# An attention block with a gated SwiGLU on one Trainium2 core: the first head's start reordered, and half of the normalised rows transposed by DMA

## The chip, the cores and the metric

The kernel runs on one core of a Trainium2 chip. The metric is the device time of an execution in microseconds (us). The core has TensorE (PE in the profile; PEld is its weight load), VectorE (DVE), ScalarE (ACT), GpSimd (POOL) and SyncE (SP), which here only issues transfers. Each engine takes its instructions in order, and engines wait for each other by semaphores. DMA transfers are issued from the queues of SP, ACT and POOL.

## The reference

A layer norm of x (2048 rows of 640) feeds an attention with 32 heads of 192 columns over a cache of 2048 keys, and a SwiGLU with 1536 hidden columns. The output joins the two:

```python
xn = _layernorm(x, axis=-1)
q = (xn @ wq).reshape(B, Sq, H, Dh).transpose(0, 2, 1, 3)
scores = jnp.einsum("bhqd,bhkd->bhqk", q, k_cache) * (Dh ** -0.5)
o = jnp.einsum("bhqk,bhkd->bhqd", softmax(scores), v_cache)
s = o.transpose(0, 2, 1, 3).reshape(B, Sq, H * Dh) @ wo
ffn = (silu(xn @ w1) * (xn @ w3)) @ w2
return x + s * silu(ffn)
```

All operands are bfloat16.

## The kernel before

**Stages.** First comes the layer norm of the 16 row tiles (128 rows each), of which tiles 0 to 3 are done before anything else and the rest inside head 0. Then the 32 heads run one after the other; each head also projects the queries of the next head. At the end come the rest of the SwiGLU and the output product. The change touches the start and head 0 only.

**Layer norm.** `ln_stats(i)` (L179) takes mean and variance of tile i on DVE; `ln_sums` (L186) does so for tiles 1 and 4 on ACT. `ln_root(i0)` (L196) makes the inverse deviations of tiles i0 and i0+1 on ACT, from the statistics of both. `ln_scale(i0)` (L214) scales the two tiles on DVE into `xn`. A *turn*, `ln_turn(i0)` (L224), transposes the two tiles on PE, ten 128x128 products by an identity into a PSUM tile `pst`, and returns the two copies from there into `xnT` (columns are rows of x); `next_turn` (L233) makes the copies on ACT.

**Projection.** `project_chunk(h, qb)` (L268) makes the queries of head h for block qb, which is 512 rows of x, or four tiles; so it needs two turns' worth of `xnT`. Head 0 uses full products of 128 rows; later heads use pairs of 64 rows, with `xnS`, a copy of `xnT` with its row halves exchanged (`swap_rows`, L298, two DMAs on POOL's queue). The PSUM tile `ps` is cast into `qA` and `qF` (DVE in head 0, ACT for head 0's first chunk and for head 1), and POOL makes `qS`, which is `qA` with its halves exchanged, and `qD` (L289, L290). `maxima()` takes the largest absolute values, from which a bound on the scores is made: DVE multiplies them with the keys' maxima and POOL sums over partitions (`bound`, L322). The bound of the very first block is made by `first_bound` (L309), with a product on PE.

**Attention.** A head has 4 blocks of 8 *pairs* of key tiles; (q, p) is pair p of block q. `advance` (L432) does one pair: `scores` (L361, six products in three steps: `qA` with `KA`, `qS` with `KB` and `KC`, `qD` and `qF` with `KC` and `KB`) into a PSUM tile, one exponential of 1024 columns on ACT (`weights`, L375) with the bound `nb` as bias, and the products with the values in two half pairs (`values`, L406; eight products each), which are queued in `parts` and lag behind by up to four halves. At the end of a block DVE reads the output banks (`evict`, L380).

**PSUM.** Scores, projections and turns share one tag, `st2`, with two buffers, which they take in program order. So the scores of a pair wait until the user two places earlier has been read: by its exponential, its casts or its copies.

**What stands where in head 0.** `advance` takes an `extra`, run on PE between pairs: before, turns at pairs 3 and 4 of block 0 (1 and 3 of blocks 1 and 2), head 0's next chunk at pair 5 (4), head 1's chunk at pair 7 (6; 1 in block 3). `posts` (L475) names layer norm steps that follow a pair. `pin` keeps an instruction's place in program order on its engine; others may be moved by the scheduler.

**Loads.** `load_keys(h)` (L102) issues on SP two transposing DMAs of the keys (`KA`, `KB`, columns 0 to 127 and 64 to 191) and the values. `load_weights(h)` (L86) issues three DMAs, for head 0 from ACT, for later heads from POOL. `copy_keys` (L116) makes `KC` on POOL by two copies and sets a column of the values to 1. `keep_busy(n)` (L175) runs n products on constants, to no other end than to keep PE busy.

Of the kernel before, what the change touches and what calls it, by code (L numbers as in the profile page):

```python
# [30 lines left out]
def _kernel_impl(ctx, tc, A_x, A_k_cache, A_v_cache, A_wq, A_wo, B_w1, B_w3, B_w2, out):  # L31
# [70 lines left out]
    def load_keys(h, mid=None):  # L102
        kh = A_k_cache[0, h]
# [3 lines left out]
        for K, c in ((KA, 0), (KB, DH - P)):  # L107
            for r in ((slice(0, HALF), slice(HALF, SK)) if h == 0 else (slice(0, SK),)):
                nc.sync.dma_start_transpose(out=K[:, r], in_=kh[r, c:c + P])  # L109
            if mid and K is KA:  # L110
                mid()
        vt = kvp.tile([P, NKT, DH + 2], BF16, tag="vt")
        nc.sync.dma_start(out=vt[:, :, 0:DH], in_=vh.rearrange("(t p) d -> p t d", p=P))
# [14 lines left out]
    with ExitStack() as actx:  # L128
# [32 lines left out]
        def load_x(eng, t0, t1):  # L161
            eng.dma_start(out=x_all[:, t0:t1, :], in_=x2[t0 * P:t1 * P, :].rearrange("(t p) d -> p t d", p=P))
# [70 lines left out]
        def next_turn(i0):  # L233
            for copy in ln_turn(i0):
                copy()

# [15 lines left out]
        keep_busy(2)  # L252
# [3 lines left out]
        def start_head(h):  # L256
            L = loads.pop(h)
            heads[h] = dict(
                h=h, L=L, vt=L["vt"],
# [8 lines left out]
        def project_chunk(h, qb, cast=nc.vector.tensor_copy):  # L268
# [21 lines left out]
            keep(nc.gpsimd.tensor_copy(out=qD[:, qs], in_=qF[PGW:P, qs]))  # L290
# [18 lines left out]
        def first_bound():  # L309
# [4 lines left out]
                                               in1=hd["st"][:, 2:4, 0], op0=ALU.mult, op1=ALU.mult))  # L314
            bp = ps_o.tile([P, 2, 512], F32, tag="ob0", name="bp")
# [45 lines left out]
        def scores(hd, qb, p):  # L361
# [7 lines left out]
            for s, step in enumerate(steps):  # L369
                for t, (k, ks, q) in enumerate(step):  # L370
# [35 lines left out]
        def values(hd, qb, p, pT2):  # L406
            vt = hd["vt"]
# [34 lines left out]
        start_head(0)  # L442
        loads[1] = load_weights(1)
        ln_sums(4)
        for s in range(2):
            for k in range(2):
                key_maxima(0, s, k, 2)
        maxima = project_chunk(0, 0, nc.scalar.copy)
        swap_rows(0)
        loads[1].update(load_keys(1))  # L450
        maxima()
        early = [scores(heads[0], 0, p) for p in range(2)]
        keep_busy(2)
        first_bound()
        keep_busy(4)
        ln_stats(5)
# [3 lines left out]
        start_head(1)  # L460
# [3 lines left out]
        def first_project(h, qb):  # L464
            maxima = project_chunk(h, qb, nc.vector.tensor_copy if h == 0 else nc.scalar.copy)
# [6 lines left out]
        def steps(*fs):  # L472
# [3 lines left out]
            (0, 1): ((ln_root, 4), (ln_stats, 6), (ln_scale, 4), (ln_stats, 7)),  # L476
            (0, 3): ((ln_root, 6), (ln_scale, 6), (ln_stats, 8), (ln_stats, 9)),
# [369 lines left out]
```

## Time and profile before

| | us |
|---|---|
| median of 3 runs (lowest, highest) | 1953.76 (1953.71, 1954.74) |
| profiled execution, its own time | 1953.86 |
| its span, first to last instruction | 1952.0 |
| PE busy in the span | 1937.1 |
| first exponential of head 0 starts | 20.92 |
| first values of head 0 start | 22.36 |
| mean granted PE clock (1 is full speed) | 0.999 |

The three costliest waits of PE in the whole span are these (columns: us in total, times, longest):

```profile
PE st L371 <- POOL qS L289: 2.2, 2, 1.9
PE fill L177 <- DVE cols L144: 1.6, 1, 1.6
PE pst L228 <- DVE xn L220: 1.5, 2, 0.9
```

An arrow points at what ended the wait. In a timeline line the first two numbers are start and duration, "x10" counts merged instructions, and brackets hold the idle time before them with what ended it. PE's durations overlap, as matmuls are pipelined; the distance between two starts says how long one occupied PE. Off the PE, a long idle time costs nothing by itself.

### The profile page before, as it was taken

How to read it: one execution, taken by the hardware profiler on the slowest of the kernel's cores; microseconds unless marked ns; L12 is line 12 of the kernel's file. 1: busy time of each engine (PE TensorE's matmuls, PEld its weight loads, DVE VectorE, ACT ScalarE, POOL GpSimd, SP SyncE). 2: the span in 40 equal slices, each digit the busy share in tenths (PEclk: the TensorE clock that was granted, in tenths of full speed). 3: DMA queues.
4: the chain of work that ended last, by engine and by line, in shares of the span. 5: the costliest groups of instructions: out<-in, count | busy, mean ns of one | idle time of the engine just before them, and what ended most of it. 6: DMA issues, size and time to landing. Idle time of an engine off the chain costs nothing.

```text
span 1952.0 us, 60577 instructions
## 1 busy us (share of the span) xinstructions
PE 1937.1 (99%) x27276; PEld 1331.6 (68%) x27276; DVE 1139.0 (58%) x2262; ACT 1219.0 (62%) x1192; POOL 441.6 (23%) x642
## 2 busy tenths in 40 slices
PE   8999999999999999999999999999999999999998
PEld 4676666667766666666666666666666666567775
DVE  7765656676666666666666666666665655531111
ACT  6777777676777777777777777777777777210000
POOL 3422222222222222222222222222222210000000
PEclk9999999999999999999999999999999999999999
DMA  9332222222233322232323222323232203938882
GB/s 208 80 83 36 73 40 71 52 70 57 60 67 63 68 63 68 56 85 64 76 54 76 54 76 46 84 46 84 46 74 38 57 10 112 269 77 137 155 153 55
DMA packets 352938, 153.52 MB, mean 79 GB/s; under 512 B 303824, under 2 KB 345776, under 8 KB 352672
## 3 DMA queue, kind: packets, MB, share of 16 engines
q1 hardware_dynamic: 337200, 117.82, 28.6%
q0 software_dynamic: 8832, 26.55, 5.5%
q10 hardware_dynamic: 6640, 5.21, 1.1%
q8 instruction: 215, 3.52, 0.8%
q14 instruction: 51, 0.42, 0.1%
HBM read 56.23 MB, written 31.98 MB: 45 GB/s over the span
## 4 chain that ended last, share of the span: by engine, by line
PE 98%; DVE 0%; DMA 0%; POOL 0%; ACT 0%; SPq 0%; issue 0%; DVEq 0%
PE obank L417 35%; PE st L371 34%; PE ps L283 14%; PE ps_s L666 11%; PE ps_f L687 3%; PE ps_gu L537 1%; PE ps L562 0%; DMA KB<-in_A_k_cache_dram 0%; PE ps L277 0%; ACT pT L377 0%; SPq L109 0%; PE fill L177 0%; POOL wq L99 0%; DVE osum L388 0%; DVE osum L387 0%
## 5 line engine op out<-in xcount | busy, mean ns | idle before, releaser
L377 ACT ACTIVATE pT<-st,nb 128x1024 bf16<-128x1024 f32 x1016 | 1130.5, 1113 | 441.7 <-PE st L371 441.0
L417 PEld LDWEIGHTS <-pT 64*128 64x128 bf16 x16384 | 719.9, 94 | 237.0 <-DVE osum L388 0.9
L417 PE MATMUL obank<-vt,pT 64*128 64x193 bf16 x16384 | 856.3, 243 | 0.4 <-DVE osum L388 0.4
L387 DVE COPY osum<-obank 128x386 f32<-128x386 f32 x256 | 142.3, 556 | 509.2 <-PE obank L417 509.0
L371 PE MATMUL st<-qA,KA 64*128 64x512 bf16 x2048 | 393.9, 376 | 2.0 <-ACT pT L377 1.1
L371 PE MATMUL st<-qS,KB 64*128 64x512 bf16 x1024 | 385.5, 376 | 1.9 <-POOL qS L289 1.9
L371 PE MATMUL st<-qD,KC 64*128 64x512 bf16 x1024 | 385.7, 377 | 0.3 <-POOL qD L290 0.3
L371 PE MATMUL st<-qS,KC 64*128 64x512 bf16 x1024 | 385.5, 376 | 0.3 <-POOL qS L289 0.3
L371 PE MATMUL st<-qF,KB 64*128 64x512 bf16 x1024 | 385.7, 377 | 0.0
L289 POOL COPY qS<-qA 64x512 bf16<-64x512 bf16 x256 | 192.4, 752 | 597.2 <-DVE qA L285 588.9
L283 PE MATMUL ps<-xnT,wq 64*128 64x512 bf16 x1240 | 288.4, 376 | 0.0
L283 PE MATMUL ps<-xnS,wq 64*128 64x512 bf16 x1240 | 286.0, 377 | 0.0
L371 PEld LDWEIGHTS <-KC 64*128 64x128 bf16 x2048 | 192.2, 94 | 119.5 <-issue 2.8
L666 PE MATMUL ps_s<-wo_sb,oT 128*128 128x320 bf16 (+2 forms) x1536 | 208.8, 299 | 0.0
L371 PEld LDWEIGHTS <-KB 64*128 64x128 bf16 x2048 | 192.9, 94 | 16.0 <-issue 0.6
L283 PEld LDWEIGHTS <-wq 64*128 64x128 bf16 x2480 | 123.8, 94 | 113.8 <-issue 0.4
L666 PEld LDWEIGHTS <-oT 128*128 128x128 bf16 x1536 | 148.2, 98 | 60.6
L394 DVE TENSOR_TENSOR ostage<-osum,rl_all 128x384 bf16<-128x384 f32 x256 | 148.3, 579 | 8.8
L388 DVE TENSOR_TENSOR osum<-osum,obank 128x386 f32<-128x386 f32 x256 | 142.6, 557 | 8.9
L371 PEld LDWEIGHTS <-KA 64*128 64x128 bf16 x2048 | 105.6, 94 | 19.0 <-issue 3.7
L671 DVE SCALAR_TENSOR_TENSOR tmp<-ps_s,g_all 128x320 f32<-128x320 f32 (+2 forms) x32 | 15.6, 487 | 176.1 <-PE ps_s L666 176.1
L99 POOL DMA_DIRECT2D wq<-in_A_wq_dram x62 | 45.5, 734 | 278.0 <-PE ps L283 265.8
(97 smaller groups left out, 1246.4 us busy)
## 6 DMA issues: line engine op xcount, KB each, us to landing
vt<-in_A_v_cache_dram SPq DMA_DIRECT2D x32, 768.0 KB, 6.2
o_scr<-ostage SPq DMA_DIRECT2D x64, 384.0 KB, 3.1
wo_sb<-in_A_wo_dram POOLq DMA_DIRECT2D x1, 7680.0 KB, 31.6
wq<-in_A_wq_dram POOLq DMA_DIRECT2D x31, 160.0 KB, 3.0
hT_scr<-hblk SPq DMA_DIRECT2D x16, 256.0 KB, 3.0
xnS<-xnT POOLq DMA_DIRECT2D x8, 320.0 KB, 6.5
xt<-in_A_x_dram POOLq DMA_DIRECT2D x16, 160.0 KB, 9.2
wq<-in_B_w_dram POOLq DMA_DIRECT2D x31, 80.0 KB, 2.6
```

The source lines that it names most:

```text
L99: keep(nc.gpsimd.dma_start(out=wq[ROWS[t], :, c0:c1], in_=w.rearrange("(s p) d -> p s d", p=DT)))
L283: pin(nc.tensor.matmul(ps[:, t * 512:(t + 1) * 512], lhsT=wq[ROWS[t], s, :], rhs=xs[ROWS[t], s // 2, qs], start=(s == 0), stop=(s == 2 * D ...
L289: keep(nc.gpsimd.tensor_copy(out=qS[ROWS[t], qs], in_=qA[ROWS[1 - t], qs]))
L371: pin(nc.tensor.matmul(st2[:, t * 512:(t + 1) * 512], lhsT=k[ROWS[t], ks], rhs=q[ROWS[t], qs], start=(s == 0), stop=(s == 2)))
L377: pin(nc.scalar.activation(out=pT2[:], in_=st2[:], func=ACT.Exp, scale=SCALE, bias=nb[:]))
L387: pin(nc.vector.tensor_copy(out=osum[:], in_=ov[:, 0, :, 0:DH + 1]))
L388: pin(nc.vector.tensor_tensor(out=osum[:], in0=osum[:], in1=ov[:, 1, :, 0:DH + 1], op=ALU.add))
L394: pin(nc.vector.tensor_tensor(out=ostage[:, b * 2:b * 2 + 2, hg * DH:(hg + 1) * DH], in0=osum[:, :, 0:DH], in1=rl.unsqueeze(2).to_broadcas ...
L417: pin(nc.tensor.matmul(acc["o"][b][:, r, (j % 2) * 256:(j % 2) * 256 + DH + 1], lhsT=pT2[ROWS[r], t * 512 + j * P:t * 512 + (j + 1) * P], ...
L537: pin(nc.tensor.matmul(ps[:, o:o + 512], lhsT=w_sb[:, c, (fl - 1) * P:fl * P], rhs=xnT[:, c, qs], start=(c == 0), stop=(c == DC - 1)))
L666: pin(nc.tensor.matmul(ps, lhsT=oT[:, k, :], rhs=wo_sb[:, k, c0:c1], start=(k == 0), stop=(k == OC - 1)))
L687: pin(nc.tensor.matmul(ps[:, pi * 512:pi * 512 + c1 - c0], lhsT=lhs[fc], rhs=w2_sb[:, fc, c0:c1], start=(fc == 0), stop=(fc == FC - 1)))
```

## The change

- `first_bound` is split. `first_product` (DVE) comes first, then PE does the scores of pair 0 with fills before its first and second step (2 and 3), the bound, and the scores of pair 1. One run of 2 fills before the first projection becomes 4.
- `qD` of head 0's first chunk is copied on ACT. The weights of head 1 are issued on POOL behind the copies that exchange the rows of `qS`, no longer ahead of them.
- Statistics, root and scaling of tiles 4 and 5 come earlier. The turns of tiles 4 to 7 stand at pairs (0,1) and (0,3), and their copies run on DVE.
- Tiles 8 to 15 (rows 1024 to 2047) have no turn: `ln_send` scales two tiles and issues a transposing DMA for each from SP, from SBUF into `xnT`, a block ahead of the projection that reads it.
- Head 0's chunks stand at pair 4 of each block; head 1's at (1,1), (2,1), (3,1) and (3,4), so its first comes a block later. Its maxima, and `swap_rows`, are placed anew.
- Keys of head 1 are loaded after (0,7), not before the first scores; its `KC` copies and the keys of head 2 follow (2,2) instead of (0,6); weights and `KC` copies of head 2 follow (3,5) instead of coming before block 3.
- Loads of x and of the keys of heads 0 to 2 are pinned.

```diff
@@ -100,17 +100,18 @@
     def load_keys(h, mid=None):
+        keep = pin if h <= 2 else (lambda x: x)
         kh = A_k_cache[0, h]
...
             for r in ((slice(0, HALF), slice(HALF, SK)) if h == 0 else (slice(0, SK),)):
-                nc.sync.dma_start_transpose(out=K[:, r], in_=kh[r, c:c + P])
+                keep(nc.sync.dma_start_transpose(out=K[:, r], in_=kh[r, c:c + P]))
             if mid and K is KA:
...
         vt = kvp.tile([P, NKT, DH + 2], BF16, tag="vt")
-        nc.sync.dma_start(out=vt[:, :, 0:DH], in_=vh.rearrange("(t p) d -> p t d", p=P))
+        keep(nc.sync.dma_start(out=vt[:, :, 0:DH], in_=vh.rearrange("(t p) d -> p t d", p=P)))
         return dict(KA=KA, KB=KB, vt=vt)
...
@@ -159,7 +160,7 @@
         def load_x(eng, t0, t1):
-            eng.dma_start(out=x_all[:, t0:t1, :], in_=x2[t0 * P:t1 * P, :].rearrange("(t p) d -> p t d", p=P))
+            pin(eng.dma_start(out=x_all[:, t0:t1, :], in_=x2[t0 * P:t1 * P, :].rearrange("(t p) d -> p t d", p=P)))
 
...
@@ -231,8 +232,13 @@
         def next_turn(i0):
-            for copy in ln_turn(i0):
+            for copy in ln_turn(i0, (nc.vector.tensor_copy, nc.vector.tensor_copy)):
                 copy()
+
+        def ln_send(i0):
+            ln_scale(i0)
+            for t, xn in enumerate(scaled.pop(i0)):
+                pin(nc.sync.dma_start_transpose(out=xnT[:, :, (i0 + t) * P:(i0 + t + 1) * P], in_=xn[:]))
 
...
@@ -249,14 +255,14 @@
             copy()
-        keep_busy(2)
+        keep_busy(4)
 
...
             heads[h] = dict(
-                h=h, L=L, vt=L["vt"],
+                h=h, L=L,
                 qA=qp.tile([P, SQ], BF16, tag="qA", name="qA"),
...
@@ -287,7 +293,10 @@
                 keep(nc.gpsimd.tensor_copy(out=qS[ROWS[t], qs], in_=qA[ROWS[1 - t], qs]))
-            keep(nc.gpsimd.tensor_copy(out=qD[:, qs], in_=qF[PGW:P, qs]))
+            if h == 0 and qb == 0:
+                keep(nc.scalar.copy(out=qD[:, qs], in_=qF[PGW:P, qs]))
+            else:
+                keep(nc.gpsimd.tensor_copy(out=qD[:, qs], in_=qF[PGW:P, qs]))
 
...
@@ -306,12 +315,16 @@
 
-        def first_bound():
+        def first_product():
             hd = heads[0]
...
                                                in1=hd["st"][:, 2:4, 0], op0=ALU.mult, op1=ALU.mult))
+            return pr
+
+        def first_bound(pr):
+            hd = heads[0]
             bp = ps_o.tile([P, 2, 512], F32, tag="ob0", name="bp")
...
@@ -358,7 +371,7 @@
 
-        def scores(hd, qb, p):
+        def scores(hd, qb, p, fill=(0, 0, 0)):
             KA, KB, KC = hd["L"]["KA"], hd["L"]["KB"], hd["L"]["KC"]
...
@@ -367,6 +380,7 @@
             for s, step in enumerate(steps):
+                keep_busy(fill[s])
                 for t, (k, ks, q) in enumerate(step):
...
@@ -404,7 +418,7 @@
         def values(hd, qb, p, pT2):
-            vt = hd["vt"]
+            vt = hd["L"]["vt"]
 
...
@@ -440,28 +454,32 @@
         start_head(0)
+        ln_sums(4)
+        for k in range(2):
+            key_maxima(0, 0, k, 2)
+        ln_stats(5)
+        ln_root(4)
+        for k in range(2):
+            key_maxima(0, 1, k, 2)
+        maxima = project_chunk(0, 0, nc.scalar.copy)
         loads[1] = load_weights(1)
-        ln_sums(4)
-        for s in range(2):
-            for k in range(2):
-                key_maxima(0, s, k, 2)
-        maxima = project_chunk(0, 0, nc.scalar.copy)
         swap_rows(0)
-        loads[1].update(load_keys(1))
         maxima()
-        early = [scores(heads[0], 0, p) for p in range(2)]
+        pr = first_product()
+        early = [scores(heads[0], 0, 0, (2, 3, 0))]
+        first_bound(pr)
+        early.append(scores(heads[0], 0, 1))
         keep_busy(2)
-        first_bound()
-        keep_busy(4)
-        ln_stats(5)
+        ln_scale(4)
         warm = stt.tile([P, 1], F32, tag="warm", name="warm")
...
 
-        start_head(1)
         all_keys = [(s, k, NQB) for k in range(NQB) for s in range(2)]
...
         def first_project(h, qb):
+            if h == 1 and qb == 0:
+                start_head(1)
             maxima = project_chunk(h, qb, nc.vector.tensor_copy if h == 0 else nc.scalar.copy)
...
@@ -473,36 +491,47 @@
         posts = {
-            (0, 1): ((ln_root, 4), (ln_stats, 6), (ln_scale, 4), (ln_stats, 7)),
-            (0, 3): ((ln_root, 6), (ln_scale, 6), (ln_stats, 8), (ln_stats, 9)),
-            (0, 5): ((ln_stats, 10), (ln_stats, 11), (ln_root, 8)),
-            (0, 7): ((ln_scale, 8), (ln_root, 10)),
-            (1, 2): ((ln_scale, 10), (ln_stats, 12), (ln_stats, 13)),
-            (1, 5): ((ln_stats, 14), (ln_stats, 15), (ln_root, 12)),
-            (1, 7): ((ln_scale, 12), (ln_root, 14)),
-            (2, 2): ((ln_scale, 14),),
+            (0, 0): ((ln_stats, 6),),
+            (0, 1): ((ln_stats, 7), (ln_root, 6), (ln_scale, 6)),
+            (0, 4): ((ln_stats, 8),),
+            (0, 5): ((ln_stats, 9), (ln_root, 8), (swap_rows, 1)),
+            (0, 6): ((ln_send, 8), (ln_stats, 10)),
+            (0, 7): ((ln_stats, 11), (ln_root, 10), (ln_send, 10)),
+            (1, 2): ((ln_stats, 12), (ln_stats, 13)),
+            (1, 4): ((ln_root, 12), (ln_send, 12)),
+            (1, 5): ((ln_stats, 14), (ln_stats, 15), (swap_rows, 2)),
+            (1, 6): ((ln_root, 14), (ln_send, 14)),
+            (2, 5): ((swap_rows, 3),),
+        }
+        extra_at = {
+            (0, 1): ((next_turn, 4),),
+            (0, 3): ((next_turn, 6),),
+            (0, 4): ((first_project, 0, 1),),
+            (1, 1): ((first_project, 1, 0),),
+            (1, 4): ((first_project, 0, 2),),
+            (2, 1): ((first_project, 1, 1),),
+            (2, 4): ((first_project, 0, 3),),
+            (3, 1): ((first_project, 1, 2),),
+            (3, 4): ((first_project, 1, 3),),
         }
...
             more = qb + 1 < NQB
-            at = (1, 3, 4, 6) if qb else (3, 4, 5, 7)
-            extras = dict(zip(at, (steps((next_turn, 4 * qb + 4)), steps((next_turn, 4 * qb + 6)),
-                                   steps((first_project, 0, qb + 1)), steps((first_project, 1, qb)))))
-            if not more:
-                extras = {1: steps((first_project, 1, qb))}
-                loads[2].update(load_weights(2))
-                copy_keys(loads[2])
             for p in range(NPAIR):
-                advance(heads[0], qb, p, extras.get(p), early.pop(0) if early else None)
-                if p == 3 and behind:
+                ex = extra_at.get((qb, p))
+                advance(heads[0], qb, p, steps(*ex) if ex else None, early.pop(0) if early else None)
+                if (qb, p) in ((2, 3), (2, 7), (3, 3), (3, 6)):
                     behind.pop(0)()
-                if p == (4 if qb else 5) and more:
-                    swap_rows(qb + 1)
-                if p == 6 and qb == 0:
+                for f, *a in posts.get((qb, p), ()):
+                    f(*a)
+                if (qb, p) == (0, 7):
+                    loads[1].update(load_keys(1))
+                if (qb, p) == (2, 2):
                     copy_keys(heads[1]["L"])
                     loads[2] = load_keys(2)
-                for f, *a in posts.get((qb, p), ()):
-                    f(*a)
+                if (qb, p) == (3, 5):
+                    loads[2].update(load_weights(2))
+                    copy_keys(loads[2])
                 if qb >= NQB - 2 and p > 3 or qb == NQB - 1 and p > 1:
```

## The prediction

> **What bounds the kernel now.** The page's top and its chain of waits come first.
>
> ```profile
> span 1952.0 us, 60577 instructions
> PE 1937.1 (99%) x27276; PEld 1331.6 (68%) x27276; DVE 1139.0 (58%) x2262; ACT 1219.0 (62%) x1192; POOL 441.6 (23%) x642
> PE 98%; DVE 0%; DMA 0%; POOL 0%; ACT 0%; SPq 0%; issue 0%; DVEq 0%
> ```
>
> TensorE is the bound from end to end, and the change touches only the start and head 0, so what counts is PE's idle time up to about 90 us and the PE work removed there. Next I read the timeline of the first 90 us, engine by engine (columns: start us, us, engine, line, operation):
>
> ```profile
> 16.35 1.29 POOL L289 COPY qS<-qA 64x512 bf16<-64x512 bf16 x2
> 20.45 0.24 PE L317 MATMUL bp<-prb,ones_bf 128*128 128x1 bf16 x2
> 20.92 2.12 ACT L377 ACTIVATE pT<-st,nbb 128x1024 bf16<-128x1024 f32 x2 [5.76 <-DVE nbb L319]
> 22.36 0.51 PE L417 MATMUL obank<-vt,pT 64*128 64x193 bf16 x8
> ...
> 40.12 0.72 PE L228 MATMUL pst<-ident_bf,xn 128*128 128x128 bf16 x10
> 41.12 0.39 PE L371 MATMUL st<-qA,KA 64*128 64x512 bf16 x2 [0.28 <-ACT pT L377]
> ```
>
> The reader sees the bound's product come 4 us after the row swaps, the first exponential 0.47 us behind it, and one turn on PE: values before it end at 39.98 (eight from 39.65 at 0.0417), so a turn takes 1.1 us with its stall. Then DVE behind a projection that ends at 32.56:
>
> ```profile
> 32.66 0.69 DVE L285 CAST qA<-ps 128x512 bf16<-128x512 f32 x1 [2.21 <-PE ps L277]
> 33.27 0.68 DVE L286 CAST qF<-ps 128x512 bf16<-128x512 f32 x1
> 33.87 0.68 DVE L294 TENSOR_REDUCE st<-qA 128x1 f32<-128x512 bf16 x1
> ...
> 35.49 0.16 DVE L327 TENSOR_REDUCE ns<-pr 128x1 f32<-128x2 f32 x1
> 35.56 0.88 DVE L183 BATCH_NORM_STATS2 st<-x_all 128x6 f32<-128x320 bf16 x2
> ...
> 37.46 0.21 DVE L184 BATCH_NORM_AGGREGATE mv<-st 128x2 f32<-128x12 f32 x1
> ```
>
> DVE has no gap here: two tiles' statistics are ready 5.1 us after the projection. Units used below, from the same timeline: scores of a pair 0.65, half a pair's values 0.333, a pair 1.315 (scores that start at 91.98 and 93.29), head 0's projection 2.25, head 1's 2.16, turn 0.7 without stall, exponential 1.03 apart and 1.16 until PE goes on, root (L207, L210) 0.45, scaling of two tiles 0.8, statistics 1.05 a tile.
>
> **Start.** KB still lands at 12.80, so DVE's maxima end at 16.6 as now. On POOL the swaps move ahead of three weight issues (13.88 to 16.35): they wait for qA (14.67) and end at 16.0, not 17.64. qD is copied on ACT (bounds 0.58, a cast, and 0.61, POOL's copy; either ends before 15.8). Pair 0's scores end at 16.7, not 18.8; the fills stand in waits. The bound's product on DVE took 0.37 and 0.61, each ending with a POOL copy (17.00, 17.65); with those copies gone it could end at 17.0, as now at 17.65. I take 17.3. PE makes the bound behind pair 0 instead of pair 1 and six fills; the first exponential starts 0.47 later, at 17.8 for 20.92. The extra statistics and root of tiles 4 and 5 lie in DVE's gap at 11.1 to 12.8 and ACT's at 13.05 to 14.09. Without that cover they cost 1.05 and 0.8.
>
> **Block 0 of head 0, to the end of head 1's first projection.** Before: values start at 22.36, scores (1,1) and their one half-pair end at 39.98; work 16.34 (8 scores 5.2, 16 halves 5.33, 2 turns 1.4, projections 4.41), stalls 1.28. After, the same work (the projection is at pair (1,1)), but new waits:
> - The two turns' copies go from ACT (1.28 a turn) to DVE. No row has 640 columns from PSUM on DVE; 386 take 0.556 and 512 take 0.69, hence about 0.75 each (0.56 to 0.83), 1.5 a turn. The root of tiles 6 and 7 stands on ACT ahead of exponential 2 and needs statistics 7, which stand behind these copies: after the first exponential's start scaling 0.8, statistics 1.05, copies from 2.05 to 3.55, statistics to 4.6, root to 5.1, exponential to 6.25. PE is out of work at 4.85, as the second turn needs the buffer: stall 1.4, and 0.35 before each of two scores.
> - The root of tiles 8 and 9 moves ahead of exponential 6, behind statistics 8 and 9, which end 5.1 after the projection (rows above). Exponentials 6 and 7 queue behind it: 6 ends at 5.15+0.45+1.16 = 6.8. PE has three scores and six halves, 3.95. Stall 2.85.
> - The root of tiles 10 and 11, behind two more statistics and a scaling, holds exponential (1,0), whose buffer head 1's projection needs: 0.85.
>
> Sum: 17.8+1.16+16.34+5.95 = 41.25, that is 1.3 later than 39.98.
>
> **Two turns gone from block 1 and two from block 2.** PE goes from 39.98 to 48.83 (end of chunk 2's projection) in 8.85; without the turns it has 3 scores, 6 halves and a projection, 6.2: -2.65. The next two do the same, 57.6 to 66.41: -2.6. Their ACT copies leave too, off the path. In their place SP transposes each tile (5 blocks of 128x128) from SBUF, a source that no row has. L109's rows (16 blocks from DRAM) are issued in 1.24 to 7.65 and land in 4.2 (least), 5.5 (median), 17.2 (most). Tiles 10, 11 are sent at 38.8, needed at 45.2: by blocks two issues of 0.65 and 4.2 make 5.5, covered; the high end, 17.2, would be 11 late. I take the first, since KA and KB of head 1 now queue behind these transposes. Tiles 12 to 15 have 7.9 us. Head 1's keys now start at about 40 and are needed by POOL at pair (2,2), about 59; head 2's at about 60, needed at 76: hidden unless they take three times the 5.5.
>
> **A root in block 1.** The root of tiles 14, 15 stands ahead of exponential (1,7), behind projection, scaling and two statistics on DVE: 6.0+0.45+1.16 = 7.6 after the projection's end, where PE has 4 scores and 8 halves, 5.26. Stall, with the wake-up, 2.45. Before, the root stood behind that exponential.
>
> **Head 1's bound.** Its weights for head 2 and KC copies move from the start of block 3 to pair (3,5), behind the last projection's swaps on POOL and ahead of the sum that gives head 1's bound.
>
> ```profile
> 74.01 0.74 POOL L99 DMA_DIRECT2D wq<-in_A_wq_dram  x1
> ...
> 76.21 1.03 POOL L118 COPY KC<-KA 64x1024 bf16<-64x1024 bf16 x1
> 77.30 1.04 POOL L119 COPY KC<-KB 64x1024 bf16<-64x1024 bf16 x1
> 78.28 0.17 POOL L120 MEMSET vt<- 128x16 bf16 x1
> ```
>
> From the projection's end: swaps 1.0 to 3.0, this group 4.44, the sum 0.4: 7.85. The exponential of (head 1, 0, 0) wants it at 5.15 and ends at 9.0; PE, at 6.6, needs its buffer for head 2's projection. Stall 2.4.
>
> **No time** I give the pins on loads, the memset in start_head (0.07), and the maxima of head 1's chunks (1.4 each on DVE), which are popped later: DVE is idle there, 2 to 4 us before the evictions and casts of blocks 1 and 2.
>
> **Sum.** +1.3 -2.65 +2.45 -2.6 +2.4 = +0.9. The profiled execution took 1953.86 (span 1952.0, 1.86 around it), so 1954.8; it stands 0.1 above the median, so 1954.7. The bounds of the bound's product move it by 0.3 either way, those of the copies by 0.4.
>
> **Rivals.**
> Slower: the stalls halve PE's clock. The view in stretches of 1 us (last three columns: granted clock, DMA share, GB/s):
>
> ```profile
> 16.00:17.00 1.00, 0.00 (x0) 0.00 (x0) 0.97 (x2) 0.00 (x0) 0.98 (x2) 1.00 1.06 338
> 17.00:18.00 1.00, 0.68 (x2) 0.18 (x2) 0.62 (x2) 0.00 (x0) 0.91 (x2) 1.00 1.06 360
> ...
> 19.00:20.00 1.00, 1.00 (x5) 0.13 (x2) 0.00 (x0) 0.00 (x0) 0.62 (x1) 0.50 1.02 262
> ```
>
> The clock was 0.50 from about 19.0 to 22.4 (0.80 in the stretch 22 to 23), after a gap of 1.9 and a thin stretch to 18.4: PE busy some 40% of 15.6 to 19.0, against 55% of the 3.4 us before. If a stall of 2.85, 2.45 or 2.4 takes most of such a window, 3.4 us at half speed lose 1.7. One gives 1956.4, two 1958.1, three 1959.8; it decides from two on. For it: the lengths. Against: work on both sides is dense. [...]
>
> Late transposes: if they land like the loads between 28 and 60 us (KB, median 10.6), tiles 10, 11 are there at 49.4, 4.2 late: 1958.9. Against: few other transfers run then. [...] The output loads' 48 blocks landing in 12.3 (0.26 a block) disagree: chance 0.02, inside the 0.10 below.
>
> Faster: the new waits on ACT, DVE and POOL don't reach PE, because statistics or POOL's group run sooner than in line. They sum to 10.3 here; all hidden 1944.5, half hidden 1949.6. Against: each engine takes its instructions in order in the rows read.
>
> **Chances.** Forecast (1952.5 to 1956) 0.45; half clock once 0.14, twice or more 0.16; late transposes 0.10; faster 0.15. What a measurement of this kernel can tell from no change is about 0.2%, 3.9 us: bounds 1949.85 and 1957.67. Faster 0.15, same 0.45+0.14 = 0.59, slower 0.26. The range, 1949.0 to 1959.8, takes in three halved windows and the half-hidden case; left out are the rest of the faster and of the late case.
>
> **What would show it.** First exponential near 17.8. ACT idle for DVE before exponentials 2, 6, (1,0) and (1,7), PE idle for ACT 1 to 3 us each; no turns after 30 us; PE idle 2.4 near the end of head 0 with POOL's sum behind KC; clock 0.5 where the slower case holds. Wrong if ACT's roots find their statistics done, or a projection waits for a DMA into xnT.

## The result, and the profile after

| | before | after |
|---|---|---|
| median, us (lowest, highest), 10 runs each | 1953.74 (1952.58, 1954.74) | 1959.22 (1956.63, 1960.26) |
| profiled execution, its span | 1953.86, 1952.0 | 1959.34, 1957.3 |

The ratio is 1.0026, with a 95% interval of 1.0017 to 1.0036: the changed kernel is slower by about a quarter of a per cent, just beyond what can be told from no change. The page of the changed kernel, its span, its busy times and its chain by engine:

```profile
span 1957.3 us, 60510 instructions
PE 1937.9 (99%) x27230; PEld 1389.2 (71%) x27239; DVE 1143.3 (58%) x2268; ACT 1214.6 (62%) x1181; POOL 443.7 (23%) x641
PE 96%; DVE 1%; DMA 1%; ACT 1%; SPq 0%; POOL 0%; issue 0%; ACTq 0%; DVEq 0%
```

PE shows 46 instructions fewer and is busy for 0.8 us longer, and the chain of waits now runs over DVE, ACT and DMAs for 1% each. So work was removed from PE, and the time came back as waits and as slower work. The first exponential starts at 17.27, for 20.92 before. Then come the waits of PE (us in total, times, longest):

```profile
PE obank L431 <- ACT pT L391: 4.7, 2, 2.6
PE ps L289 <- ACT pT L391: 2.5, 1, 2.5
...
PE ps L289 <- DMA wq<-in_A_wq_dram: 0.9, 1, 0.9
```

The timeline of ACT shows who kept ACT from serving PE: two roots (L208) that wait for DVE's statistics, with exponentials queued behind them, and an exponential that waits for POOL's sum.

```profile
32.58 0.29 ACT L208 ACTIVATE lv<-mv,eps_t 128x2 f32<-128x2 f32 x1 [3.17 <-DVE mv L185]
33.01 2.10 ACT L391 ACTIVATE pT<-st,nbb 128x1024 bf16<-128x1024 f32 x2
...
52.81 0.30 ACT L208 ACTIVATE lv<-mv,eps_t 128x2 f32<-128x2 f32 x1 [2.26 <-DVE mv L185]
...
89.44 2.12 ACT L391 ACTIVATE pT<-st,nb 128x1024 bf16<-128x1024 f32 x2 [3.01 <-POOL nb L343]
```

On PE the same three places are idle times of 2.62, 2.04 and 2.46 us, and at the third one more wait follows, for the weights of head 2:

```profile
34.16 0.82 PE L431 MATMUL obank<-vt,pT 64*128 64x193 bf16 x8 [2.62 <-ACT pT L391]
...
54.40 0.60 PE L431 MATMUL obank<-vt,pT 64*128 64x193 bf16 x8 [2.04 <-ACT pT L391]
...
90.61 0.37 PE L289 MATMUL ps<-xnT,wq 64*128 64x512 bf16 x1 [2.46 <-ACT pT L391]
91.86 0.39 PE L289 MATMUL ps<-xnS,wq 64*128 64x512 bf16 x2 [0.88 <-DMA wq<-in_A_wq_dram]
```

And in stretches of 1 us (third number from the end: the granted clock of PE) each of the three is followed by 3.4 us at half speed. Here are the first and the second:

```profile
33.00:34.00 1.00, 0.00 (x0) 0.00 (x0) 0.86 (x3) 1.00 (x2) 0.00 (x0) 1.00 1.07 197
34.00:35.00 1.00, 0.83 (x10) 0.74 (x12) 0.97 (x4) 1.00 (x2) 0.00 (x0) 0.60 0.85 225
35.00:36.00 1.00, 1.00 (x6) 0.30 (x4) 0.94 (x3) 0.12 (x1) 0.00 (x0) 0.50 0.90 152
36.00:37.00 1.00, 1.00 (x14) 0.89 (x12) 0.43 (x2) 0.96 (x3) 0.00 (x0) 0.50 0.97 134
37.00:38.00 1.00, 1.00 (x14) 0.66 (x12) 0.78 (x3) 0.54 (x1) 0.00 (x0) 0.69 0.87 165
...
53.00:54.00 1.00, 0.00 (x0) 0.00 (x0) 0.62 (x2) 0.97 (x3) 0.00 (x0) 1.00 1.09 193
54.00:55.00 1.00, 0.60 (x10) 0.55 (x12) 0.18 (x1) 1.00 (x2) 0.00 (x0) 0.84 0.87 252
55.00:56.00 1.00, 1.00 (x7) 0.31 (x4) 0.92 (x2) 0.35 (x1) 0.00 (x0) 0.50 1.77 157
```

PE is full in the slow stretches (1.00 busy); what it does there takes twice as long: the steps of a pair's scores start 0.43 us apart at 35 us, and 0.22 at 38. The third lies at 92.2 to 95.6. Before, there was one such stretch, around the start of the first exponential (19.0 to 22.4).

Five marks on PE, each the start of the scores behind a projection (the first and third in before are the same places in the work), give the time by stage. The last column is a second profile of the changed kernel, told of below, in which the clock was never halved up to 104 us:

| stage ends at | before | after | after, full clock |
|---|---|---|---|
| block 0, head 1's first projection | 39.98 | 40.63 | 39.49 |
| chunk 2's projection | 48.83 | 46.93 | 45.89 |
| pair (2,1) | 57.56 | 59.56 | 56.84 |
| chunk 3's projection | 66.41 | 65.87 | 63.15 |
| head 2's first projection | 90.18 | 95.37 | 90.78 |

At 63 to 66 us the changed kernel is still ahead; all that it loses, and more, it loses between there and head 2's first projection.

### The profile page after: what moved, and what is told of

Same layout as the page of the kernel before. It is cut to its first block, busy times and chain, and to the rows that moved or that the text cites. A ratio compares the mean times of both kernels' runs of the same rounds, so it can differ in the third digit from the quotient of the medians.

```text
span 1957.3 us, 60510 instructions
## 1 busy us (share of the span) xinstructions
PE 1937.9 (99%) x27230; PEld 1389.2 (71%) x27239; DVE 1143.3 (58%) x2268; ACT 1214.6 (62%) x1181; POOL 443.7 (23%) x641
## 4 chain that ended last, share of the span: by engine, by line
PE 96%; DVE 1%; DMA 1%; ACT 1%; SPq 0%; POOL 0%; issue 0%; ACTq 0%; DVEq 0%
PE obank L431 34%; PE st L385 33%; PE ps L289 14%; PE ps_s L695 11%; PE ps_f L716 3%; PE ps_gu L566 1%; DMA wq<-in_A_wq_dram 1%; PE ps L591 0%; PE ps L283 0%; DMA vt<-in_A_v_cache_dram 0%; SPq L110 0%; ACT pT L391 0%; DVE st L303 0%; DVE st L184 0%; DMA x_all<-in_A_x_dram 0%
## 5 line engine op out<-in xcount | busy, mean ns | idle before, releaser
L431 PEld LDWEIGHTS <-pT 64*128 64x128 bf16 x16384 | 747.2, 94 | 214.7 <-ACT pT L391 5.1
L431 PE MATMUL obank<-vt,pT 64*128 64x193 bf16 x16384 | 869.7, 243 | 5.2 <-ACT pT L391 4.7
L385 PE MATMUL st<-qA,KA 64*128 64x512 bf16 x2048 | 406.9, 377 | 1.0 <-ACT pT L391 0.6
L289 PEld LDWEIGHTS <-wq 64*128 64x128 bf16 x2480 | 139.4, 94 | 105.4 <-DMA wq<-in_B_w_dram 3.8
L385 PEld LDWEIGHTS <-KA 64*128 64x128 bf16 x2048 | 118.6, 94 | 16.2 <-issue 3.1
```

The costliest lines, as they stand in the source:

```text
L289: pin(nc.tensor.matmul(ps[:, t * 512:(t + 1) * 512], lhsT=wq[ROWS[t], s, :], rhs=xs[ROWS[t], s // 2, qs], start=(s == 0), stop=(s == 2 * D ...
L385: pin(nc.tensor.matmul(st2[:, t * 512:(t + 1) * 512], lhsT=k[ROWS[t], ks], rhs=q[ROWS[t], qs], start=(s == 0), stop=(s == 2)))
L431: pin(nc.tensor.matmul(acc["o"][b][:, r, (j % 2) * 256:(j % 2) * 256 + DH + 1], lhsT=pT2[ROWS[r], t * 512 + j * P:t * 512 + (j + 1) * P], ...
```

## The experiments

Each but the last ran in several executions beside the kernel before, whose median was 1953.96 in the first group of four, 1953.54 in the second and 1953.56 in the third. The edits are against the changed kernel unless said otherwise.

### The waits on DVE and on POOL, taken away one at a time and together

Statistics of tiles 8 to 15 earlier, so that the roots find them done:

```diff
-            (0, 4): ((ln_stats, 8),),
-            (0, 5): ((ln_stats, 9), (ln_root, 8), (swap_rows, 1)),
...
+            (0, 3): ((ln_stats, 8), (ln_stats, 9)),
+            (0, 4): ((ln_stats, 10), (ln_stats, 11)),
...
-            (1, 5): ((ln_stats, 14), (ln_stats, 15), (swap_rows, 2)),
+            (1, 2): ((ln_stats, 12), (ln_stats, 13), (ln_stats, 14), (ln_stats, 15)),
+            (1, 5): ((swap_rows, 2),),
```

> The changed kernel with only the places of statistics moved: those of tiles 8 and 9 to pair (0,3), 10 and 11 to (0,4), 14 and 15 to (1,2), so that each root on ACT finds them done. Theory A (roots on ACT wait for DVE, PE waits behind them, and each long stall halves PE's clock for 3.4 us): the stalls of 2.6 and 2.0 us before the last values of blocks 0 and 1 go, with some 1.6 us for each halved window, 7.8 in all: 1951.4 (1950.3 to 1953). Theory B (the DMA transposes or the late loads of head 1 cost the time): no change, 1959.2.

Measured: 1954.16 (1950.83 to 1957.19), ratio 1.0001 (0.9992 to 1.0010), 2.8 above what was expected. The idle times behind the roots were gone, and the two slow stretches with them, but chunk 2's projection found its rows missing. PE's timeline and SP's queue in this run:

```profile
43.12 2.32 PE L283 MATMUL ps<-xnT,wq 128*128 128x512 bf16 x10 [1.98 <-ACT rstd L211]
```

```profile
33.50 6.43 SPq L241 DMA_TRANSPOSE xnT<-xn  x4
```

The line names an ACT root that ended 0.7 us before and belongs to tiles 12 and 13, which this projection does not read. What ends at that time is the last of SP's four transposes of tiles 8 to 11, which take 6.4 us to issue: its issue ends at 39.9, and its data land at 43.03. So the late transposes were a real cost in this profile, which the stalls of the changed kernel had covered (there PE came to this projection at 44.67). They are not always so late: in the run with both edits, told of below, whose instructions are the same up to there, the last landed at 41.06, and PE waited 0.31 us.

Weights and `KC` copies of head 2 back at the start of block 3:

```diff
+            if not more:
+                loads[2].update(load_weights(2))
+                copy_keys(loads[2])
             for p in range(NPAIR):
...
-                if (qb, p) == (3, 5):
-                    loads[2].update(load_weights(2))
-                    copy_keys(loads[2])
```

> The changed kernel with only the weights and KC copies of head 2 put back to the start of block 3. Theory A: head 1's bound and head 2's weights are ready in time, the idle stretch of 3.7 us at 88 to 92 us and its halved window (1.6) go: 1953.9 (1953 to 1955). Theory B: no change, 1959.2.

Measured: 1951.97 (1950.81 to 1954.41), ratio 0.9991 (0.9982 to 1.0000). That is 7.2 below the changed kernel's median, and 1.0 below the range that was expected. The boundary's idle time and its slow stretch are gone. The two idle times behind the roots stayed, 2.62 and 2.04, in this profile each with its slow stretch; but three of the eleven executions had a mean clock of 1.000, at 1950.81 to 1951.53, where the profiled one had 0.998, so in these the slow stretches were gone as well.

Both edits:

> Both edits. Theory A: the gains add, 7.8 and 5.3: 1946.1 (1945 to 1948), 0.4% below the kernel before, no halved window after the start. Theory B: 1959.2. If the stalls hide each other: between, 1949 to 1952.

Measured: 1950.00 (1947.26 to 1952.13), ratio 0.9979 (0.9970 to 0.9988): by the median better than either alone, 4 us short of the expectation. PE came to chunk 3's projection so early that the transposes of tiles 12 to 15 were late, and the slow stretch behind that wait came too. The timelines of PE and SP, and PE's clock, in this run:

```profile
60.23 1.04 PE L283 MATMUL ps<-xnT,wq 128*128 128x512 bf16 x2 [3.89 <-DMA xnT<-xn]
```

```profile
46.88 10.95 SPq L241 DMA_TRANSPOSE xnT<-xn  x4
```

```profile
60.00:61.00 1.00, 0.77 (x2) 0.28 (x3) 0.00 (x0) 0.00 (x0) 0.00 (x0) 0.50 1.20 247
61.00:62.00 1.00, 1.00 (x4) 0.39 (x3) 0.00 (x0) 0.00 (x0) 0.00 (x0) 0.50 1.09 227
```

Four transposes took 10.95 us on SP, and the first landed 11.3 us after its issue began. Head 1's keys had landed by 47.4; what was in flight beside the transposes is head 1's values (until 50.9) and the row swaps sent from 47.2 (until 58.2). In the changed kernel two transposes sent at 37.1 and 38.5, with only transposes in flight, took 1.2 us each to issue and 2.6 to land; two sent at 51.8 and 54.1, behind row swaps sent at 50.8 and 51.5, took 2.2 and 2.8 to issue and 7.7 and 6.0 to land. That the row swaps slow them is a reading of these traces; no run takes the swaps away.

### Are the DMA transposes worth anything?

The run with both edits, with tiles 8 to 15 turned on PE again and their copies on ACT:

```diff
-            (0, 6): ((ln_send, 8),),
+            (0, 6): ((ln_scale, 8),),
...
+            (1, 2): ((act_turn, 8),),
+            (1, 3): ((act_turn, 10),),
...
+            (2, 2): ((act_turn, 12),),
+            (2, 3): ((act_turn, 14),),
```

> Both edits, and tiles 8 to 15 turned on PE again (at pairs (1,2), (1,3), (2,2), (2,3), copies on ACT) instead of by DMA. Theory A: four turns of 0.7 to 1.1 us come back on PE: 2.8 to 4.4 above the run with both edits. Theory B (the DMA transposes cost time): faster than the run with both edits.

Measured: 1949.11 (1947.96 to 1952.29), ratio 0.9977 (0.9967 to 0.9988): 0.9 below the run with DMA transposes, which the spread of the runs does not tell from none; 2.8 to 4.4 above was expected. A turn put on PE costs what it should (0.87 us by the stages below), but the late transposes and the slow stretch left with the DMAs. The profile had a new gap, in which PE waited for nothing that it shows, with SP's queue in the middle of head 1's keys:

```profile
32.32 0.37 PE L389 MATMUL st<-qS,KB 64*128 64x512 bf16 x1 [1.52 <-issue]
```

```profile
19.92 11.41 SPq L110 DMA_TRANSPOSE KB<-in_A_k_cache_dram  x1
```

Without the sends nothing holds SP's queue, so these keys go over 20 us sooner than in the changed kernel. To see whether the gap hangs on them, one pair of sends was put back, which makes the keys queue behind it:

```diff
-            (0, 6): ((ln_scale, 8),),
+            (0, 6): ((ln_send, 8),),
...
-            (1, 2): ((act_turn, 8),),
```

> Statistics early and the weights and key copies of head 2 at block 3's start, tiles 10 to 15 turned on TensorE, only tiles 8 and 9 sent by DMA transposes. With all tiles turned on TensorE the span was 1948.0, with 1.5 us in which TensorE stood at 30.8-32.3 although nothing that the profile shows was awaited, while SP's queue was transposing head 1's keys KB (19.9-31.4). Here the two sends hold SP's queue until about 33, so head 1's keys go behind them. Theory M (that gap comes from the key transposes on the DMA engines): no such gap, and one turn of 0.7 us less on TensorE: span 1945.5-1946.5, median 1947-1948. Rival N (the gap has nothing to do with the keys): gap of about 1.5 us again, span about 1947.3, median 1948.5. Rival L (tiles 8 and 9 land late, or the keys of head 1 come late for it): up to 2 us idle ahead of chunk 2's projection at 41 us or at the change to head 1 near 60, median 1949-1951.

Measured: 1947.50 (1947.15 to 1948.76), ratio 0.9969 (0.9958 to 0.9980), the fastest of all. The gap is gone, and between the ends of the projections the stage of block 0 took 9.09 us for 10.55, the next one 7.25 for 8.12 (a turn less). The start of this execution lost 1.2 us to a load of weights, hence the span of 1947.0 where 1945.5 to 1946.5 was expected. The gap goes with the keys' place here, but not with that alone: the kernel before issues the same `KB` at 21.86, in 7.65 us, and shows no such gap, while the start by itself, told of below, issues it at 19.73, in 11.09 us, and has a gap of 0.86. Whether keys in flight stop PE's issue, and by what way, is not shown.

Transposes of tiles 12 and 13 sent one pair sooner, those of 14 and 15 two, with their statistics ahead of them and the keys of head 1 behind them (against the run with both edits):

```diff
...
-            (1, 4): ((ln_root, 12), (ln_send, 12)),
+            (1, 3): ((ln_root, 12), (ln_send, 12)),
+            (1, 4): ((ln_root, 14), (ln_send, 14)),
...
-            (1, 6): ((ln_root, 14), (ln_send, 14)),
...
-                if (qb, p) == (0, 7):
+                if (qb, p) == (1, 5):
```

> The run with both edits (e3_both), in which the projection of chunk 3 waited 3.9 us for the DMA transposes of tiles 12 to 15, with the cause of that taken away if it is SP's queue: roots, scaling and transposes of tiles 12 to 15 two pairs earlier, and the loads of head 1's keys and values behind them instead of ahead. Theory D (the transposes were late behind the key loads): no wait before chunk 3, no halved window there: 1950.0 - 3.9 - 1.6 = 1944.5 (1943.5 to 1946.5). Theory E (a transpose from SBUF is slow by itself): the wait stays above 2 us, 1948 to 1950.

Measured: 1952.61 (1946.00 to 1955.24), ratio 0.9989 (0.9978 to 0.9999), a miss. The transposes were in time, but now the keys of head 2, which queue behind those of head 1, were late and in the way. PE's waits in this run, and POOL's timeline:

```profile
PE ps L289 <- DMA xnS<-xnT: 4.4, 1, 4.4
```

```profile
79.54 1.04 POOL L120 COPY KC<-KB 64x1024 bf16<-64x1024 bf16 x1 [11.36 <-DMA KB<-in_A_k_cache_dram]
```

These keys, issued from 57.9, were in flight together with the row swaps for head 1's projection, the second of which took 13.3 us to land, at 77.57, and with head 2's weights (13 us); `KB` itself took 15.5. The 4.4 us wait was followed by two slow stretches, 75.5 to 82.3.

### What holds PE at the head boundary

The `KC` copies alone behind POOL's sum, weights as in the changed kernel:

```diff
                     loads[2].update(load_weights(2))
-                    copy_keys(loads[2])
...
                 finish_head(1)
+                copy_keys(loads[2])
```

> The changed kernel with the KC copies of head 2 moved behind the sum that gives head 1's bound; head 2's weights stay at pair (3,5). If the late bound alone holds PE at 88 us: 1953.5 to 1955. If the late weights hold it in turn (they landed at 91.7 us): the idle stretch stays near 3.7 us and the time at 1958 to 1959.5. I expect the second.

Measured: 1956.97 (1954.64 to 1959.40), ratio 1.0017 (1.0008 to 1.0025). The sum now came at 86.05 and its exponential in time, and PE waited all the same, 3.21 us for the weights alone (PE's waits):

```profile
PE ps L289 <- DMA wq<-in_A_wq_dram: 3.2, 1, 3.2
```

The wait is the one that was expected; the median is 1 us below the expected range. In this profile no slow stretch follows the wait, for a reason told below.

The weights alone back at the start of block 3, the `KC` copies left where they are:

```diff
+            if not more:
+                loads[2].update(load_weights(2))
...
-                    loads[2].update(load_weights(2))
                     copy_keys(loads[2])
```

> The changed kernel with only the weights of head 2 put back to the start of block 3; the KC copies stay at pair (3,5), ahead of the sum. The sum then ends 2.2 us earlier, at about 87.2 for 89.4, and PE waits less than 0.5 us at the end of head 0, no halved window: 1953.5 to 1955. If the KC copies hold the bound as much as the weights did: above 1956.

Measured: 1953.54 (1951.36 to 1955.27), ratio 0.9998 (0.9989 to 1.0006), as expected. PE's idle time at the boundary fell to 0.40. In this profile, at 1951.36 the fastest of its twelve, the idle times of 2.62 and 2.04 us are in place, and no slow stretch follows either, for the same reason. So the weights are the cause twice over: their three issues hold POOL's sum back by 2.2 us, and their data land too late. In the changed kernel the third was issued at 85.61 and took 6.12 us, beside head 3's keys that SP issues from 84.83 (chain of waits):

```profile
85.61 6.12 DMA wq<-in_A_wq_dram
91.86 4.00 PE ps L289 x19
```

### The start by itself

The kernel before, with only the start of the change (bound's product between the first two pairs, weights of head 1 behind the row swaps, `qD` on ACT, fills):

```diff
-        loads[1] = load_weights(1)
...
+        loads[1] = load_weights(1)
         swap_rows(0)
...
-        early = [scores(heads[0], 0, p) for p in range(2)]
-        keep_busy(2)
-        first_bound()
-        keep_busy(4)
+        pr = first_product()
+        early = [scores(heads[0], 0, 0, (2, 3, 0))]
+        first_bound(pr)
+        early.append(scores(heads[0], 0, 1))
+        keep_busy(2)
```

> The kernel before with the start part of the change alone (row swaps ahead of the weights on POOL, first qD on ACT, bound between the scores of pairs 0 and 1, fills moved); loads, turns, statistics and places in head 0 as before. Theory A (the start gives its 3.65 us, 20.92 to 17.27 for the first exponential, and all of the loss lies in the later waits): 1950.3 (1949 to 1952). Theory C (the start's gain is lost anyway, as the layer norm of tiles 4 to 7 catches up with it): 1952.5 to 1954.

Measured: 1952.06 (1949.60 to 1963.04), ratio 0.9998 (0.9986 to 1.0010). In the profiles the first exponential starts at 16.71, 4.2 sooner. Chunk 1's projection ends 4.5 sooner, those from head 1's first to 70 us end 2.75 sooner, and those from head 1's last on 1.50, as that one waited 1.27 us for its row swaps. The median lies between the two expectations, 1.5 below that of the kernel before, which agrees with the 1.50; but the interval does not exclude nothing.

### When the clock is halved

One statistic less ahead of each root:

```diff
-            (0, 4): ((ln_stats, 8),),
+            (0, 3): ((ln_stats, 8),),
...
-            (1, 2): ((ln_stats, 12), (ln_stats, 13)),
+            (1, 2): ((ln_stats, 12), (ln_stats, 13), (ln_stats, 14)),
...
-            (1, 5): ((ln_stats, 14), (ln_stats, 15), (swap_rows, 2)),
+            (1, 5): ((ln_stats, 15), (swap_rows, 2)),
```

> The changed kernel with one statistic of each pair moved ahead (tile 8's behind pair (0,3), tile 14's behind pair (1,2)), so that one statistic of 0.9-1.0 us less stands ahead of each square root. Both theories: exponential 6's stall falls from 2.62 to about 1.6 us and that of pair (1,7) from 2.04 to about 1.0. Theory G (the clock is granted for a stretch of 3.41 us by TensorE's idle time in the stretch before; the traces so far: 1.83 us idle or less, full clock; 2.01 us or more, half): no half clock at 30-60 us whatever the phase; only the stall of 2.46 + 0.88 us at the head boundary can still halve one. Profiled span 1950.2 without a half stretch, 1951.9 with one; median 1953.5-1954.5. Rival H (every stall beyond some 1 us is answered by half a clock): two half stretches at 30-60 us, span about 1955, median 1957. Rival L (the transposes by DMA become late when TensorE comes to chunk 2 sooner, as they were by 1.98 us when all statistics were early): 0.5-1.5 us idle ahead of chunk 2's projection near 41 us, and the median that much above G's.

Measured: 1954.80 (1953.23 to 1956.67), ratio 1.0008 (0.9999 to 1.0017). The idle times were 1.63 and 1.05, and no stretch at half clock followed them; the one in this profile follows the boundary's idle time. No projection waited for transposes. The median is 0.3 above the expected span of values.

The same with weights and `KC` copies early:

> As the run with half of the statistics moved ahead, with the weights and key copies of head 2 back at block 3's start as well. Theory G: no stretch at half clock in any phase unless the transposes of tiles 12 to 15 come more than 1.9 us late; without a late transpose the span is 1945.7 (that of the run with weights and copies early, 1951.1, less its two half stretches of 1.7 us and less 2.0 us of stall), with transposes late by half of the 3.9 us seen when all statistics were early 1947.6: median 1947.7-1949.6, and a narrower spread than the 3 to 4 us of the changed kernel. Rival L: chunk 3's projection waits 3 us or more, with a half stretch behind it: span 1949.5-1950.5, median 1951-1952.

Measured: 1950.08 (1948.84 to 1950.78), ratio 0.9981 (0.9972 to 0.9990). The highest and lowest of 11 runs are 1.9 us apart, for 3.6 in the changed kernel, and the profile has no half stretch before 1944 us and no late transpose. The median is 0.5 above the expected ones; what this half microsecond is stays open.

The changed kernel once more, in one execution, nothing edited:

> The changed kernel once more, for another phase of the clock's stretches. Theory G: the edges of the half stretches lie on a grid of 3.413 us that stands elsewhere than in the first profile (34.21 + n x 3.413), and a stretch is half exactly where the one before held 2.0 us or more of idle TensorE: one, two or three of them (for phases spread evenly in about 1, 10 and 9 of 20 executions), span about 1953.8, 1955.5 or 1957.2. Rival H (every stall of 2 us or more is followed by half a clock at once): always three, behind each of the three stalls, span 1957.0-1957.5.

Measured: 1954.45, span 1952.4, where the kernel before had 1953.56 beside it, with idle times of 2.62, 2.04 and 2.45 + 0.57 us in the same three places and no half stretch at all. PE's waits (0.62 of the second line's 3.1 lie at 37.3), and the stretches of 1 us around the first:

```profile
PE obank L431 <- ACT pT L391: 4.7, 2, 2.6
PE ps L289 <- ACT pT L391: 3.1, 2, 2.5
```

```profile
32.00:33.00 1.00, 0.00 (x0) 0.00 (x0) 0.37 (x3) 0.65 (x3) 0.44 (x1) 1.00 0.70 143
33.00:34.00 1.00, 0.09 (x2) 0.09 (x4) 1.00 (x3) 1.00 (x2) 0.00 (x0) 1.00 0.99 184
34.00:35.00 1.00, 1.00 (x18) 0.65 (x19) 0.96 (x4) 0.86 (x1) 0.00 (x0) 1.00 1.01 254
```

That kills the rival that any stall of 2 us is answered by half a clock. It was also outside the shares given for the other theory, which had one to three half stretches: those were worked out from a trace in which half stretches had stretched the distance between the stalls. So the same kernel takes 1954.45 without a half stretch and 1959.34 with three.

The traces with a half stretch show where these lie. In the changed kernel's they begin at 34.21, 54.69 and 92.23, the second and third 6 and 17 times 3.413 us behind the first. Behind PE's last work the clock falls to half as well, in the changed kernel at 1955.91; that is 545 times 3.4133 behind the end of its third half stretch, 95.65. In the kernel before it falls at 1950.92, 565 times 3.4133 behind the end of its half stretch, 22.39. So in both traces this fall lies on the grid too, and it is taken to locate the grid in a trace that has no half stretch. In the unhalved profile it falls at 1950.43, which puts edges at 32.15, 52.62 and 86.76 (562, 556 and 546 times 3.4133 sooner): they cut all three waits. The view of the unhalved profile in stretches of that grid (second number: busy time of PE), with the fall behind the last work:

```profile
28.73:32.15 3.42, 2.56 (x44) 1.62 (x38) 3.25 (x10) 0.42 (x1) 2.87 (x5) 1.00 0.03 5
32.15:35.56 3.41, 1.65 (x30) 1.30 (x32) 2.74 (x9) 2.51 (x4) 0.29 (x1) 1.00 0.95 195
...
86.76:90.17 3.41, 1.72 (x15) 0.76 (x16) 0.70 (x2) 3.38 (x4) 2.98 (x4) 1.00 1.26 243
1950.00:1951.00 1.00, 0.00 (x0) 0.00 (x0) 0.00 (x0) 0.00 (x0) 0.00 (x0) 0.72 0.00 0
```

So the wait of 2.62 us came as 0.86 and 1.76, and no stretch held more than 1.76 us of idle time. Laying the grid over each trace from 10 to 104 us gives, for all stretches in which PE was idle for more than 1.5 us:

| idle in a stretch of 3.413 us | next stretch | where |
|---|---|---|
| 1.58 | full | before |
| 1.63 | full | half of the statistics early, in both runs |
| 1.69, 1.76 | full | changed kernel, unhalved profile |
| 1.71 | full | statistics early (of the 1.98 us wait) |
| 1.81 | full | `KC` behind the sum (of the 3.21 us wait) |
| 1.91 | full | weights early (of the 2.04 us wait) |
| 2.04 | half | changed kernel, and two other runs |
| 2.05 | half | before, the start |
| 2.15 to 2.67 | half | eight more, in six traces |
| 3.41 | half | both edits |

(The expectations above have 2.01 and 1.83 for the 2.05 and the 1.81.) The 3.21 us wait is the telling one. An edge at 89.41, known from that trace's other half stretches, cut it into 1.40 and 1.81 us, and the clock stayed full; a wait of 2.04 us inside one stretch halved it. The stretch, not the wait, is what counts here, and in a second execution of the same kernel the grid lies elsewhere (edges at 34.21 and at 32.15). The limit lies between 1.91 and 2.04 us idle in these traces. The runs bear out the price: the mean granted clock was 0.998 in three of the changed kernel's ten runs, with a mean of 1957.94, and 0.997 in seven, with 1959.39 (a profile with two half stretches has 0.998, the one with three 0.997); with the 1954.45 at 1.000, a single execution, three half stretches cost 4.9 us, 1.65 each.

## Why the prediction came out as it did

The time lay inside the range, but the likeliest case did not happen; the slower rival did, with three halved stretches in the profiled execution; the prediction gave a slower outcome 0.26. The forecast's own sum, which leaves the clock at full speed, can be held against the profile without half stretches (that of the kernel before has its one, at 19.0 to 22.4):

| term | predicted | full clock | profiled after |
|---|---|---|---|
| start and block 0 | +1.3 | -0.49 | +0.65 |
| two turns gone, block 1 | -2.65 | -2.45 | -2.55 |
| root in block 1 | +2.45 | +2.22 | +3.90 |
| two turns gone, block 2 | -2.6 | -2.54 | -2.54 |
| head 1's bound | +2.4 | +3.86 | +5.73 |
| sum | +0.9 | +0.60 | +5.19 |

(differences of the five marks above). The time at full clock, 1954.45, is close to that of the sum, 1954.8 for the profiled execution, but in part by luck: start and block 0 came out 1.8 below the prediction and the head boundary 1.5 above it. Two of its additions are off besides: the stalls listed for block 0 make 5.80, where the sum takes 5.95, and all the waits listed make 10.65, where the faster rival takes 10.3.

- **The step that failed is the weight given to the half clock.** The prediction had the half clock behind a stall, its stretch of 3.4 us and its price (1.7; measured 1.65), and its case of three such stretches, 1959.8, is what most runs show. It gave this less chance than the unhalved sum, on the argument that work on both sides is dense. The density of the neighbours did not matter: 2.04 us idle inside one stretch of 3.413 were enough, so each of the stalls of 2.62, 2.04 and 2.46 + 0.88 us can halve it, and the granted clock of the ten runs says that mostly they did. Read that way, the rows of before spoke plainly: 2.05 us idle in the stretch ahead of its half stretch.
- **Start: right, a little too careful.** 17.27 for the predicted 17.8. The product and its second step took 0.17 and 0.16 us once POOL's copies no longer lay beside them.
- **Turn copies: mis-sized.** 0.49 us each on DVE, below the lower bound of 0.56 (the line says 0.89 for both, which overlap), so PE's stall before the second turn was 0.49 and not 1.4. The rows that the prediction went by read float32 from PSUM (386 columns in 0.56 us, 512 in 0.69); these copies read 640 columns of bfloat16. No run tells the type from the rest.

```profile
19.19 0.89 DVE L230 COPY xnT<-pst 128x640 bf16<-128x640 bf16 x2
```

- **Roots: right.** 2.62 for 2.85, and 2.04 for 2.45. The runs with early statistics show the cause: move the statistics and these stalls go. The third, 0.85 ahead of head 1's first projection, was 0.62 at full clock, and none in the halved profile, where PE came there later.
- **Head boundary: right place, wrong size and half the cause.** The bound's wait was 2.46 for 2.4. That the weights themselves would be late was not seen: moving them to pair (3,5) puts their landing beside head 3's keys. With the `KC` copies out of the way PE waited 3.21 us for them; with the weights early and the copies in place it waited 0.40. And one term that the prediction put at nothing had a cost in this stage, the maxima of head 1's chunks: with those of the keys they fill DVE from 67.7 to the reading of the output banks at 70.3, ahead of which DVE was idle for 2 us in before, and PE waits 0.53 us for that reading. Here are PE at full clock, and DVE before.

```profile
73.40 1.01 PE L431 MATMUL obank<-vt,pT 64*128 64x193 bf16 x20 [0.53 <-DVE osum L402]
```

```profile
74.37 0.56 DVE L387 COPY osum<-obank 128x386 f32<-128x386 f32 x1 [2.00 <-PE obank L417]
```

- **Transposes: right only by luck.** They were covered in the changed kernel, as forecast, but they took 1.2 to 2.8 us each to issue on SP, not 0.65, and the stalls gave them time. As soon as PE stalled less, they were late for chunk 2 (1.98 us in one profile, 0.31 in two others) and 3.89 for chunk 3. The 0.02 that the prediction sets inside its 0.10 was for transposes far later than that, by an estimate of the author's that no run shows. By the traces a turn of ten blocks took 0.87 us of PE, and a tile's five blocks sent by DMA landed in 2.6 us at the least and 7.7 at the most in the changed kernel. With all four pairs back on TensorE the time could not be told from that with the DMAs; the fastest run here has three of the four there.
- **Faster rival: wrong.** The big waits were not hidden from PE; only the copies were shorter, and the root's wait of 0.85 vanished in the halved profile.

## What to carry to other kernels

Where PE is the bound, price a stall twice: by its length, and by whether 2 us or more of idle time can fall into one stretch of 3.413 us (the limit in these traces lies between 1.91 and 2.04). Here each such stretch cost 1.65 us more, and stalls cut to 1.63 us lost that surcharge. Before moving a load to a later point, look at which transfers will be in flight there, and what stands behind its issues on the same queue. When one stall is removed, ask what it was covering: here three of the cures (all statistics early, both edits, the sends first) exposed a transfer that a stall had given time.

## What the hardware showed that was not expected

- The same kernel took 1954.45 us with no half stretch and 1959.39 on average with three, by where its stalls fell on the clock's grid: at most 1.76 us idle in a stretch of 3.413 us in the one, 2.04 and more in three of them in the other's profile.
- A DMA transpose of one tile (five blocks of 128x128) from SBUF took 1.2 to 2.8 us of SP's queue in the changed kernel, and 10.95 us for four beside row swaps and a load of values.
- Small DVE instructions that had ended with a POOL copy, at 0.37 and 0.61 us, took 0.17 and 0.16 without one beside them.
- PE stood for 1.52 us without a wait in the profile while SP's queue transposed head 1's keys, and did not with these keys later, nor in the kernel before; why is open.
